# Two-stage kernel on one core: halved first loads, squares by ScalarE, and a newly searched order of all steps

## The chip, the cores and the metric

The kernel runs on one core of one Trainium2 chip. A core has a matrix engine (TensorE, PE in the profile, with its weight loads as PEld), a vector engine (VectorE, DVE), an engine for activations (ScalarE, ACT), a general one (GpSimd, POOL) and one that here only issues DMAs (SyncE, SP). Each engine works through its own list of instructions in order; semaphores make one engine wait for another. The metric is the device time of one execution in microseconds (us); lower is better.

## The reference

Attention over chosen blocks, followed by a Fourier mix and a two-layer network with one activation. The inputs are q, k and v (4 batches, 8 heads, 768 positions, 64 wide, float32), and two weight matrices (512 x 2048 and 2048 x 512).

```python
k_rep = k.reshape(B, H, 12, 64, D).mean(axis=3)          # one mean key for each block of 64
gate = einsum('bhsd,bhnd->bhsn', q, k_rep), future blocks at -1e9
mask = (block is own or among the top 3 of gate) and causal
attn = softmax(where(mask, q k^T / 8, -1e9));  x = attn v  # heads side by side: 4 x 768 x 512
u  = x + real(fft2(x))                                    # over positions and over the 512 columns
un = (u - mean(u)) / sqrt(var(u) + 1e-6)                  # over the 512 columns
out = u + relu(un @ w_ch1) @ w_ch2
```

## The kernel before

Two heads of one batch make a pair; there are 16 pairs, four to a batch. For each pair the kernel turns q and k (for pairs 0 to 6 by PE transposes, for the later ones by DVE transposes), sums k over blocks, finds for each query the third largest gate score, and turns the comparison into a mask that is added to the scores by matmuls. The scores are held transposed (keys on partitions) in six tiles for a pair, and ScalarE takes their exponential; GpSimd cuts the causal diagonal; a second matmul with v and a column of ones gives the result and the sum.

When the four pairs of a batch are done, the Fourier part follows: folds (additions and subtractions on DVE), a cosine and sine transform over positions (`y`), copies by ACT or DVE (`ty`, `tr`), a transform over columns (`m`), then u = x + that, its mean and variance, a scaled copy of u, and its transpose `unT`. W1 and W2 follow. For batches 0 and 1 W2 is a plain product; for batches 2 and 3 it is done in seven block products in place of eight (sums and differences of blocks on DVE: steps `T` and `S`, products `p`, additions `po`).

No loop sets the order. A long string, `ORDER`, holds one word for each step of each pair, batch and tile, and a loop at the end calls the steps in that order; each engine's own order follows from it. `name:numbers` is a step with its pair or batch and tile, `@n` says which of a few buffers it takes, and `~` picks the other of the two engines that a step knows (for `qc`, `qs`, `vc`, `qm`, `qn`: ACT in place of DVE or GpSimd). The words that matter here:

- `Lq`, `Lk`, `Lv`: loads by SP. `tq`, `tk`: PE transposes of q and k (`a_tp`, L320); `tj`: of the last third of k of pair 0 (`b_tp`, L327).
- `ks`, `kj`: sums of k over blocks on DVE (L390, L331). `qc`: copy of q in float32 (L239 on ACT, L241 on DVE); `qs`, `kc`, `kd`: q and k as float16.
- `g`, `gj`: gate matmuls (L433, L344). `gt`, `tg`, `gx`, `xg`, `gl`, `lg`, `gm`, `mg`: turning, top three, comparison and turning back on DVE. `g`, `gt`, `gx`, `go`, `gl`, `gm` serve the first five of pair 0's nine gated blocks of 64 queries (for other pairs all of them), `gj`, `tg`, `xg`, `og`, `lg`, `mg` its other four.
- `s`, `e`, `d`: scores (L527, L532, with the mask's matmuls at L539), exponential (L549), diagonal (L555). `vc`: v as float16. `v`, `x`: attention times v (L567) and its division (L250).
- `fs`, `fd`, `f`, `fe`: folds. `y`, `ty`, `tr`, `m`, `u` (L691): the transform and u with its sum of a row. `bn`, `nv`, `nr`: statistics of a row, first guess of the inverse root and its refinement. `xu`, `xv`: scaled copy. `xt`, `un`: transpose, on PE for batch 0, by transposing DMAs on SP (L742) for the others.
- `w`, `r`: W1 and its relu (L801, L803; L811, L813). `c`, `o`: W2 of batches 0 and 1 (L820, L826). `od`: store (L832).

`consts_first` stands ahead of the string. It issues the loads of pair 0 (L903: q in two DMAs, one on SP and one on ACT's queue, then k likewise), makes constants on GpSimd and DVE, and lets PE run eight matmuls on a tile of zeros (L914). q of pair 0 is turned as a whole, k in two parts of four and two blocks of 128 rows.

The variance of all batches comes from `n_stats` (two instructions on DVE for each of six tiles of a batch, L747 and L748), and `n_guess` reads it.

Of the kernel before, what the change touches and what calls it, by code (L numbers as in the profile page):

```python
# [11 lines left out]
FP = mybir.dt.float32  # L12
F16 = mybir.dt.float16
# [93 lines left out]
Lq:1@1 Lk:1@1 tq:0@1 Lk:2@2 tk:0@2 ~qc:0@0 tj:0@3 ks:0 Lq:2@2 kj:0 kc:0 g:0@0 gj:0@1 kd:0 gt:0  # L107
tq:1@2 ~qs:0 tg:0 Lq:3@0 gu:0 xg:0 tk:1@0 og:0 gx:0 ~qc:1@1 go:0 lg:0 gl:0 mg:0@0 s:0,5@3 gm:0
s:0,2@1 ks:1 Lk:3@0 qs:1 e:0,5@0 s:0,4@2 e:0,2 ~kc:1 g:1@3 e:0,4 s:0,1@1 gt:1 s:0,0@0 ~gu:1 e:0,1
tk:2@3 gx:1 d:0,4 tq:2@2 go:1 gl:1 e:0,0 Lv:0@0 ks:2 s:0,3@1 Lq:4@1 ~qc:2@0 gm:1@1 tq:3@0 ~kc:2  # L110
e:0,3 qs:2 g:2@2 Lk:4@1 s:1,2@3 gt:2 ~qc:3@1 s:1,0@1 ~gu:2 tk:3@2 gx:2 e:1,2@1 qs:3 go:2 s:1,1@0
ks:3 e:1,0 d:0,2 s:1,4@3 Lv:1@1 d:0,5 ~kc:3 d:0,3 e:1,1 Lq:5@2 vc:0 tq:4@1 e:1,4 g:3@2 d:0,0 qc:4@0
d:0,1 Lk:5@2 s:1,3@0 gl:2 s:1,5@3 ~qs:4 tk:4@1 gt:3 gm:2@2 e:1,3 ~gu:3 v:0@2 d:1,4 ks:4 e:1,5 gx:3
kc:4 s:2,3@0 vc:1 go:3 x:0 s:2,0@3 e:2,3@0 Lv:3@0 s:2,4@1 d:1,5 d:1,3 e:2,0 g:4@2 gl:3 d:2,3 fs:0,1
Lv:2@1 tq:5@0 fs:0,0 e:2,4 gm:3@3 d:2,0 Lk:7@0 gt:4 d:1,0 tk:5@3 d:1,2 ~qc:5@1 d:1,1 s:2,5@2 ~kc:5
s:2,1@1 d:2,4 e:2,5 s:2,2@0 ~gu:4 e:2,1 vc:3 ks:5 v:1@2 e:2,2 qs:5 gx:4 s:3,5@1 go:4 s:3,0@3 gl:4
e:3,5@1 d:2,2 x:1 s:3,2@0 e:3,0 Lq:6@0 d:3,5 g:5@1 vc:2 e:3,2 s:3,3@2 gt:5 Lk:6@1 d:2,1 gm:4@0
s:3,1@3 d:3,0 gu:5 s:3,4@1 e:3,3 gx:5 d:2,5 v:2@0 d:3,2 kb:7 LT:0 e:3,1 W:0 Lq:7@1 fs:1,0 ~go:5
e:3,4 s:4,4@2 x:2 d:3,1 s:4,2@3 d:3,3 e:4,4@0 s:4,0@1 d:3,4 gl:5 v:3@0 fs:2,0 gm:5@1 e:4,2 fs:2,1
fs:1,1 e:4,0 s:5,2@2 x:3 s:4,5@3 e:5,2@1 s:4,1@1 fd:2,1 s:4,3@0 fs:3,0 e:4,5 s:5,3@2 fs:3,1 e:4,1  # L120
fd:2,0 s:5,5@3 fd:3,1 e:5,5 tq:6@1 fd:3,0 e:4,3 ~fe:0,3 s:5,0@3 f:0,2 e:5,3 tk:6@0 ~fe:0,0 ~fe:0,2
f:0,0 ~qc:6@0 s:5,4@2 LF:0 f:0,1 fe:0,1 ks:6 e:5,4 y:0,0@1 qs:6 Lv:4@0 f:0,3 e:5,0 Lc:0 pg:0 ks:7
d:4,0 g:6@2 d:4,1 ty:0,0 d:4,2 y:0,1@3 gt:6 Lv:5@1 d:4,5 ~tr:0,0 d:5,2 gu:6 gx:6 Lk:8@2 d:4,3
s:5,1@2 W:1 go:6 gl:6 ~tr:0,1 qc:7@1 m:0,2@1 vc:4 ty:0,1 gm:6@2 d:4,4 kc:6 m:0,0@3 d:5,0 u:0,2@0
d:5,4 e:5,1 Lk:9@1 d:5,3 v:4@0 qs:7 u:0,0@1 xu:0,2 s:6,4@1 xv:0,2 x:4 vc:5 m:0,1@2 kh:7 e:6,4@0
d:5,5 s:6,1@3 u:0,1@2 d:5,1 s:6,3@0 e:6,1 xt:0,2@1 ~xu:0,0 g:7@2 xv:0,0 ~xu:0,1 v:5@3 e:6,3 gt:7
un:0,2 ~gu:7 W:2 ~xv:0,1 xt:0,0@2 s:6,5@1 un:0,0 xt:0,1@0 e:6,5 s:6,0@1 un:0,1 Lq:9@2 s:6,2@2 e:6,0
x:5 w:0,8@0 d:6,0 bn:0,0 w:0,1@1 r:0,8 gx:7 kc:7 go:7 w:0,5@3 gl:7 gm:7@3 K:7 kb:8 w:0,6@0 r:0,5
ks:8 r:0,1 bn:0,3 w:0,3@3 r:0,6 d:6,3 bn:0,5 e:6,2 w:0,12@1 r:0,3 Lq:8@0 s:7,5@0 s:7,0@2 ~r:0,12
e:7,5@1 s:7,4@3 kh:8 e:7,0 s:7,3@0 fs:4,1 w:0,0@1 qc:9@0 e:7,4 Li:0 Lv:6@0 kb:9 e:7,3 w:0,10@2 qs:9  # L130
# [24 lines left out]
v:10@3 fs:11,1 r:1,8 Lv:12@1 d:12,1 fs:11,0 s:13,5@0 s:13,3@1 x:10 e:13,5@0 w:1,11@2 e:13,3 d:13,5
fs:10,1 fd:11,1 s:13,1@0 r:1,11 fd:11,0 s:13,2@3 fs:10,0 w:1,7@1 e:13,1 fd:10,1 go:14 fd:10,0
e:13,2 gl:14 s:13,4@2 f:2,2 w:1,3@0 ~fe:2,0 e:13,4 gm:14@2 d:13,2 ~fe:2,3 f:2,3 d:13,1 kh:15
w:1,14@3 f:2,1 r:1,7 K:14 qc:15@1 s:12,4@2 r:1,14 ~fe:2,2 f:2,0 w:1,0@1 e:12,4 nv:1 s:13,0@3 fe:2,1
~r:1,3 y:2,0@2 e:13,0 ~r:1,0 d:13,0 s:12,2@0 d:13,3 pg:2 g:15@3 e:12,2 d:13,4 y:2,1@1 gt:15 vc:13
tr:2,0 d:12,0 s:12,3@3 Lv:14@0 gu:15 nr:1 gx:15 ty:2,0 c:1,0,0@0 go:15 gl:15 e:12,3 ~ty:2,1 v:13@2  # L160
~tr:2,1 ~qs:15 m:2,0@3 d:12,3 x:13 d:12,2 qs:14 m:2,2@1 gm:15@3 kc:15 u:2,0@0 c:1,1,0 d:12,4 d:12,5
bn:2,0 vc:12 s:14,1@2 u:2,2@2 s:14,0@3 K:15 c:1,0,1 e:14,0@0 bn:2,4 e:14,1 bn:2,1 s:14,2@1 d:14,0
bn:2,5 s:14,4@3 e:14,2 c:1,1,1 e:14,4 ~vc:14 v:12@2 o:1,1 o:1,0 od:1,1 s:15,0@1 nv:2,2 od:1,0
s:15,5@3 c:1,4,0@0 e:15,5@1 e:15,0 xu:2,2 x:12 d:15,0 s:15,3@3 d:14,2 s:14,3@1 nv:2,0 un:2,2 e:15,3
c:1,4,1 fs:13,1 e:14,3 xu:2,0 d:15,3 fs:13,0 d:14,4 s:14,5@2 d:14,1 m:2,1@3 o:1,4 e:14,5 d:15,5
s:15,1@1 od:1,4 u:2,1@1 d:14,3 s:15,2@2 e:15,1 c:1,5,0 bn:2,2 e:15,2 d:15,1 d:14,5 bn:2,3 s:15,4@3
# [30 lines left out]
def kernel(  # L197
# [34 lines left out]
    def pick(a, b):  # L232
        return b if other[0] else a
# [778 lines left out]
```

## Time and profile before

| | us |
|---|---|
| median of 3 runs (lowest, highest) | 277.81 (277.69, 278.2) |
| the profiled execution | 277.79 |
| its span in the trace | 276.1 |
| PE busy | 267.9 |
| DVE busy | 221.5 |
| ACT busy | 178.3 |
| POOL busy | 107.4 |

The span runs from the first instruction of the program to the last one; the time of the execution is 1.7 us more. Busy time is the time in which at least one instruction of an engine runs. Rows of a group name the line, engine and operation, what is written and read, the shape and the count; then busy time in us and the mean length of one in ns, then how long the engine stood still just before these and what ended that.

### The profile page before, as it was taken

What the parts mean: (1) busy time and instruction counts of PE and PEld (TensorE: products, weight loads), DVE (VectorE), ACT (ScalarE), POOL (GpSimd) and SP (SyncE); (2) the same over time, 40 slices, a digit from 0 to 9 for tenths busy, and PEclk for the clock granted to TensorE, in tenths of its full rate; (3) what the DMA queues carried; (4) which work ended last, traced back from release to release, by engine and by line L of the source; (5) the groups of instructions that cost most, each with busy time, mean ns of one, the idle gap of its engine ahead of it and who ended that gap; (6) DMA issues with size and microseconds to landing.
All of it is one profiled execution on the core that took longest, in us unless ns stands there. A gap on an engine that the chain in (4) does not pass through costs nothing.

```text
span 276.1 us, 7004 instructions
## 1 busy us (share of the span) xinstructions
PE 267.9 (97%) x2660; PEld 181.2 (66%) x2660; DVE 221.5 (80%) x683; ACT 178.3 (65%) x243; POOL 107.4 (39%) x304
## 2 busy tenths in 40 slices
PE   8899989999999999999999999999999999999995
PEld 4566766765576565666665755655766888666884
DVE  1888999998789889899789797879999894307883
ACT  3799999969999759978799687802546310274100
POOL 5155927634783476405976691520100011000000
PEclk9999999999999999999999999999999999999999
DMA  8999999998799999479471202351100412300025
GB/s 190 271 229 235 186 233 207 180 153 151 134 174 189 168 188 194 115 124 234 119 149 29 57 2 78 77 105 51 38 2 0 59 19 68 127 0 2 0 112 194
DMA packets 121138, 33.47 MB, mean 121 GB/s; under 512 B 113616, under 2 KB 118160, under 8 KB 121104
## 3 DMA queue, kind: packets, MB, share of 16 engines
q1 hardware_dynamic: 115872, 28.43, 48.1%
q0 software_dynamic: 3664, 4.19, 9.8%
q10 hardware_dynamic: 1568, 0.39, 0.6%
q8 instruction: 21, 0.34, 0.5%
q14 instruction: 13, 0.11, 0.1%
HBM read 28.55 MB, written 6.29 MB: 126 GB/s over the span
## 4 chain that ended last, share of the span: by engine, by line
PE 81%; DVE 6%; ACT 5%; POOL 2%; issue 2%; SPq 2%; DMA 1%; DVEq 0%; ACTq 0%; POOLq 0%
PE h L801 19%; PE cw L879 13%; PE c L820 12%; PE h L803 9%; PE sc L532 7%; PE av L567 5%; PE tp L320 2%; ACT pt L549 2%; PE yp L639 2%; PE sc L527 2%; PE mx L672 2%; SPq L742 2%; PE mx L673 2%; PE sc L539 1%; PE warmps L914 1%
## 5 line engine op out<-in xcount | busy, mean ns | idle before, releaser
L549 ACT ACTIVATE pt<-sc 128x1024 f16<-128x1024 f32 (+1 forms) x96 | 83.4, 925 | 12.1 <-PE sc L532 8.1
L801 PE MATMUL h<-unT,w 128*128 128x512 f16 x256 | 84.6, 379 | 0.3 <-DMA unT<-x 0.3
L803 PE MATMUL h<-unT,w 128*128 128x256 f16 x256 | 69.7, 272 | 0.0
L813 ACT ACTIVATE hT<-h 128x768 f16<-128x768 f32 x50 | 39.4, 811 | 41.1 <-PE h L803 40.7
L555 POOL TENSOR_SCALAR_AFFINE_SELECT pt<-pt 128x256 f16<-128x256 f16 x96 | 37.4, 413 | 21.0 <-ACT pt L549 19.9
L820 PE MATMUL c<-w_sb,hT 128*128 128x512 f16 x192 | 44.5, 379 | 0.0
L801 PEld LDWEIGHTS <-w 128*128 128x128 f16 x256 | 25.0, 98 | 29.7 <-issue 1.4
L820 PEld LDWEIGHTS <-hT 128*128 128x128 f16 x192 | 18.3, 98 | 20.3 <-issue 0.5
L253 POOL TENSOR_SCALAR_AFFINE_SELECT qk<-mt 32x160 f16<-32x160 f16 x72 | 23.9, 353 | 18.2 <-DVE mt L504 16.7
L803 PEld LDWEIGHTS <-w 128*128 128x128 f16 x256 | 25.0, 98 | 3.6
L532 PE MATMUL sc<-qk 96*128 96x512 f16 (+3 forms) x144 | 26.1, 305 | 0.0
L567 PEld LDWEIGHTS <-pt 128*128 128x128 f16 x672 | 22.3, 97 | 3.2 <-ACT pt L549 0.7
L567 PE MATMUL av<-v,pt 128*128 128x65 f16 x672 | 23.2, 193 | 0.3 <-ACT pt L549 0.3
L253 POOL TENSOR_SCALAR_AFFINE_SELECT qk<-q 64x768 f16<-64x768 f32 (+1 forms) x15 | 12.3, 822 | 22.8 <-ACT q L239 15.3
L886 DVE SCALAR_TENSOR_TENSOR u<-cw,rt,u 128x256 f32<-128x256 f32 x35 | 16.6, 480 | 4.7 <-PE cw L879 4.1
L879 PEld LDWEIGHTS <-s 128*128 128x128 f16 x192 | 18.8, 98 | 2.2
L532 PEld LDWEIGHTS <-qk 96*128 96x128 f16 x144 | 13.1, 98 | 7.8
L811 DVE TENSOR_SCALAR hT<-h 128x768 f16<-128x768 f32 x14 | 13.3, 956 | 4.0 <-PE h L803 3.9
L879 PE MATMUL cw<-w2t,s 128*128 128x256 f16 x144 | 16.4, 273 | 0.0
L250 DVE TENSOR_TENSOR s<-hT,hT 128x384 f16<-128x384 f16 x16 | 5.4, 354 | 13.4 <-ACT hT L813 13.3
L250 DVE TENSOR_TENSOR x<-av,rcp 128x768 f16<-128x768 f32 x16 | 15.3, 958 | 0.6
L879 PEld LDWEIGHTS <-hT 128*128 128x128 f16 x144 | 14.1, 98 | 2.0
(155 smaller groups left out, 457.2 us busy)
## 6 DMA issues: line engine op xcount, KB each, us to landing
nat<-in_v_dram SPq DMA_DIRECT2D x16, 384.0 KB, 4.6
out_dram<-u SPq DMA_DIRECT2D x20, 256.0 KB, 2.4
nat<-in_k_dram SPq DMA_DIRECT2D x36, 96.0 KB, 3.4
nat<-in_q_dram SPq DMA_DIRECT2D x36, 96.0 KB, 2.9
nat<-in_q_dram SPq DMA_DIRECT2D x13, 192.0 KB, 3.7
nat<-in_k_dram SPq DMA_DIRECT2D x13, 192.0 KB, 3.9
w_sb<-in_moe_w_ch_dram POOLq DMA_DIRECT2D x2, 1024.0 KB, 11.2
w<-in_moe_w_ch_dram POOLq DMA_DIRECT2D x2, 768.0 KB, 7.1
```

The source lines that it names most:

```text
L250: (eng or nc.vector).tensor_tensor(out=out, in0=in0, in1=in1, op=op)
L253: nc.gpsimd.affine_select(out=out, in_=in_, pattern=[[0, i] for i in n], base=0, channel_multiplier=0, compare_op=ALU.is_ge, fill=0.0)
L532: nc.tensor.matmul(ps[:, e, co:co + q1 - q0], qk[0:96, e, 1, 128 * jt:128 * jt + 128], qk[0:96, e, 0, q0:q1], start=True, stop=True)
L549: nc.scalar.activation(out=d["pt"][:, o:o + 2 * n].rearrange("p (e c) -> p e c", e=2), in_=d["sc", i][:, :, 0:n], func=AF.Exp, scale=0.125)
L555: nc.gpsimd.affine_select(out=dg, in_=dg, pattern=[[0, 2], [1, 128]], base=0, channel_multiplier=-1, compare_op=ALU.is_ge, fill=0.0)
L567: nc.tensor.matmul(av[:, e, 66 * st:66 * st + 65], pt[:, co:co + 128], vv[:, e, jt, 0:65], start=(cnt == 0), stop=(cnt == 20))
L801: nc.tensor.matmul(hp[:, 0:512], w1s, unT[:, dt, 0:512], start=(dt == 0), stop=(dt == NDT - 1))
L803: nc.tensor.matmul(hp[:, 512:768], w1s, unT[:, dt, 512:768], start=(dt == 0), stop=(dt == NDT - 1))
L813: nc.scalar.activation(out=hT, in_=hp, func=AF.Relu)
L820: nc.tensor.matmul(c_ps[b, g[0]][:, st - g[0], :], h_t[b, it][:, 128 * st:128 * (st + 1)], w2_sb[:, it, :], start=(it == 0), stop=(it == N ...
L879: nc.tensor.matmul(o, x, y, start=(i == 0 and W7_FIRST[n]), stop=(i == 7), skip_group_check=True)
L886: nc.vector.scalar_tensor_tensor(out=o, in0=c_ps[b, "w", st][:, W7_BANK[n], 0:256], scalar=rt_t[b][:, kt:kt + 1], in1=o, op0=ALU.mult, op1 ...
```

## The change

The change has four parts.

1. **First pair.** q of pair 0 is loaded and turned in two parts as k is: eight DMAs in place of four, first four blocks of 128 rows of k and of q (each on SP and ACT's queue), then the other two blocks of k and q, all on SP. New steps `tn`, `qn` and `qm` turn and copy the second part of q; `tq`, `qc` and `qs` of pair 0 handle 512 columns. k now comes ahead of q.
2. **Warm-up.** The tile of zeros is 128 columns wide and read four times by each matmul; there are seven matmuls in place of eight, and the copy that reads their result moves to the end of DVE's constants.
3. **Variance of batches 2 and 3.** `bn` is replaced by two steps: `mn` scales the sum of a row that `u` left to minus the mean (DVE, two columns at a time), and `sq` lets ACT square u minus mean and sum the row; the squares themselves are written over x, which is not read any more. `n_guess` divides the sum by 512. Batches 0 and 1 keep `bn`.
4. **Order.** All steps stand in a new order, with other buffers and other choices of engine here and there: q of pair 4 is copied by ACT in place of DVE, two casts of v move from GpSimd to ACT, one copy of `tr` from DVE to ACT, two relus from ACT to DVE.

```diff
     def a_tp(P, who):
-        two = P == 0 and who == 1
+        two = P == 0
...
+    def b_tq(P):
+        pairs[P]["tpn"] = ps = pst([128, 256], f"tpn_{P}")
+        src = nat[P, 0].rearrange("p st e d -> p st (e d)")
+        for st in range(4, NST):
+            nc.tensor.transpose(ps[:, 128 * st - 512:128 * st - 384], src[:, st, :], id32)
+
+    def b_q32(P):
+        conv(pick(nc.vector, nc.scalar), q_tile(P)[:, 512:S], pairs[P]["tpn"], None)
+
+    def b_q(P):
+        conv(pick(nc.gpsimd, nc.scalar), qk_s[P % NSLOT][:, 0, XW(P), 512:S], q_tile(P)[:, 512:S], [S - 512])
...
+    def n_mean(b, kp):
+        sm = st_t[b][2][:, 2 * kp:2 * kp + 2]
+        nc.vector.tensor_scalar(out=sm, in0=sm, scalar1=-1.0 / DM, scalar2=None, op0=ALU.mult)
+
+    def n_square(b, kt):
+        nc.scalar.activation(out=x_t[b][:, kt, :], in_=u_t[b, kt // 2][:, kt % 2, :], func=AF.Square,
+                             bias=st_t[b][2][:, kt:kt + 1], accum_out=st_t[b][0][:, kt, 1:2])
...
-            nc.vector.tensor_scalar(out=vr, in0=mv[:, :, 1], scalar1=1e-6, scalar2=None, op0=ALU.add)
+            nc.vector.tensor_scalar(out=vr, in0=ss, scalar1=1.0 / DM, scalar2=1e-6, op0=ALU.mult, op1=ALU.add)
...
-            nc.vector.scalar_tensor_tensor(out=nm, in0=mv[:, :, 0], scalar=-1.0, in1=g,
-                                           op0=ALU.mult, op1=ALU.mult)
+            tt(nm, nm, g, ALU.mult)
...
-            for e, eng in ((0, nc.sync), (1, nc.scalar)):
-                eng.dma_start(t[:, :, e, :], src[0, e].rearrange("(st p) d -> p st d", p=128))
+        for h in (slice(0, 4), slice(4, NST)):
+            for who in (1, 0):
+                src = (q, k)[who]
+                for e, eng in ((0, nc.sync), (1, nc.sync if h.start else nc.scalar)):
+                    eng.dma_start(nat[0, who][:, h, e, :],
+                                  src[0, e].rearrange("(st p) d -> p st d", p=128)[:, h, :])
...
-        for _ in range(8):
-            nc.tensor.matmul(wps, wsrc[:, 0:128], wsrc, start=True, stop=True)
+        for _ in range(7):
+            nc.tensor.matmul(wps.rearrange("p (r c) -> p r c", c=128), wsrc, wsrc.rearrange(
+                "p (r c) -> p r c", r=1).to_broadcast([128, 4, 128]), start=True, stop=True)
```

The head of the order, before and after:

```diff
-Lq:1@1 Lk:1@1 tq:0@1 Lk:2@2 tk:0@2 ~qc:0@0 tj:0@3 ks:0 Lq:2@2 kj:0 kc:0 g:0@0 gj:0@1 kd:0 gt:0
-tq:1@2 ~qs:0 tg:0 Lq:3@0 gu:0 xg:0 tk:1@0 og:0 gx:0 ~qc:1@1 go:0 lg:0 gl:0 mg:0@0 s:0,5@3 gm:0
+tk:0@1 Lq:1@1 tq:0@2 ks:0 Lk:1@1 tj:0@3 ~qc:0@0 kj:0 Lk:2@2 ~qs:0 g:0@0 tn:0@2 gt:0 ~qn:0 gu:0 gx:0
+Lq:2@2 kc:0 gj:0@0 go:0 gl:0 ~qm:0 tg:0 kd:0 gm:0@0 s:0,0@2 xg:0 Lq:3@0 og:0 tk:1@1 e:0,0@0 lg:0
```

The stretch in which batch 2 passes from attention to W1, before and after:

```diff
-s:15,1@1 od:1,4 u:2,1@1 d:14,3 s:15,2@2 e:15,1 c:1,5,0 bn:2,2 e:15,2 d:15,1 d:14,5 bn:2,3 s:15,4@3
-d:15,2 v:14@1 nv:2,1 e:15,4 ~xu:2,1 c:1,5,1 d:15,4 un:2,1 nr:2 v:15@2 o:1,5 T:2 od:1,5 c:1,2,0@3
-un:2,0 x:14 c:1,2,1 x:15 fs:12,1 fs:12,0 c:1,3,0 fs:14,1 fs:14,0 fs:15,1 fs:15,0 fd:14,1 fd:15,1
+m:2,1@1 e:15,3 un:2,2 c:1,5,0 e:15,1 u:2,1@1 s:15,2@0 mn:2,1 fs:13,0 s:14,5@2 c:1,5,1 e:14,5 e:15,2
+d:14,5 d:15,2 s:15,4@1 o:1,5 v:14@2 e:15,4 d:15,3 od:1,5 od:1,4 sq:2,3 c:1,2,0@0 d:15,4 un:2,0
+d:15,1 sq:2,2 d:15,5 nv:2,1 v:15@3 nr:2 ~xu:2,1 x:14 un:2,1 c:1,2,1 fs:14,1 x:15 c:1,3,0 fs:15,1
```

## The prediction

> **What bounds the kernel now.** I read the page's first part, then busy time by stage, the chain that ended last, the waits, and the start row by row.
>
> ```profile
> span 276.1 us, 7004 instructions
> PE 267.9 (97%) x2660; PEld 181.2 (66%) x2660; DVE 221.5 (80%) x683; ACT 178.3 (65%) x243; POOL 107.4 (39%) x304
> ```
>
> ```profile
> core 0: us, PE busy (x) PEld busy (x) DVE busy (x) ACT busy (x) POOL busy (x), PEclk, DMA share, GB/s
> 11.01:35.58 24.57, 23.62 (x412) 16.85 (x410) 22.09 (x84) 23.78 (x30) 16.44 (x41) 1.00 1.02 229
> 35.58:58.00 22.42, 21.15 (x368) 16.10 (x363) 21.31 (x64) 20.85 (x31) 11.03 (x24) 1.00 1.06 184
> ...
> 150.00:178.79 28.79, 28.79 (x291) 18.46 (x290) 23.75 (x77) 22.50 (x28) 17.48 (x49) 1.00 0.19 52
> ```
>
> ```profile
> 58.00:272.85 214.85, 214.24 (x1832) 142.78 (x1830) 172.83 (x508) 128.99 (x178) 75.74 (x216) 1.00 0.48 96
> 272.85:276.09 3.24, 0.00 (x0) 0.00 (x0) 0.48 (x1) 0.00 (x0) 0.00 (x0) 1.00 0.53 185
> ```
>
> The cuts are events: 11.01 is the first exponential, 35.58 the end of the last one of the first batch (e:3,4), 58.00 the first W1 matmul. Ahead of 58.00 PE is fed by others: ACT has 23.78 of 24.57 us filled between 11.01 and 35.58, and DVE 21.31 of 22.42 after that. From 58.00 on PE is filled to 214.24 of 214.85, and 3.24 us of last addition and store follow. So the time is a sum: first W1 matmul, plus the PE work behind it, plus PE's idle time there (0.61), plus the tail. The change leaves the matmuls behind the first W1 matmul as they are (in the built order the same PE work stands ahead of it, but for one warm-up matmul less). It can only move the first W1 matmul, and the 0.61.
>
> The profiled execution took 277.79 us, 1.7 over its span; the median of the runs is 277.81. I sum against 277.79.
>
> **The start.** Each row is start, length, engine, line, operation.
>
> ```profile
> 0.82 0.47 ACTq L903 DMA_DIRECT2D nat<-in_q_dram  x1
> 1.31 3.59 PE L914 MATMUL warmps<-zeros 128*128 128x512 f16 x8 [1.31 <-DVE zeros L911]
> 1.32 0.69 ACTq L903 DMA_DIRECT2D nat<-in_k_dram  x1
> 1.94 1.14 SPq L304 DMA_DIRECT2D nat<-in_q_dram  x2
> 4.69 2.34 PE L320 MATMUL tp<-id,nat 128*128 128x128 f32 x10
> 6.22 0.80 ACT L239 COPY q<-tp 128x768 f32<-128x768 f32 x1 [2.68 <-PE tp L320]
> 7.14 0.69 DVE L390 TENSOR_REDUCE kra<-tp 128x8 f32<-128x512 f32 x1 [1.18 <-PE tp L320]
> 7.87 0.59 ACT L239 CAST qk<-tp 128x512 f16<-128x512 f32 x1 [0.85 <-DVE kra L390]
> 7.98 0.48 PE L433 MATMUL g<-q,kra 64*32 64x160 f32 x8 [0.53 <-DVE kra L390]
> 8.35 0.38 ACT L239 CAST qk<-tpj 128x256 f16<-128x256 f32 x1
> 8.51 0.35 DVE L448 STREAM_TRANSPOSE gt<-g 128x160 f32<-128x160 f32 x1 [0.27 <-PE g L433]
> 8.74 1.53 PE L320 MATMUL tp<-id,nat 128*128 128x128 f32 x12
> 9.65 0.80 ACT L239 COPY q<-tp 128x768 f32<-128x768 f32 x1 [0.20 <-PE tp L320]
> 10.62 0.30 DVE L502 STREAM_TRANSPOSE mt<-lt 128x160 f16<-128x160 f16 x1
> 11.01 4.19 ACT L549 ACTIVATE pt<-sc 128x256 f16<-128x256 f32 x5 [0.55 <-PE sc L539]
> ```
>
> ```profile
> nat<-in_q_dram ACTq DMA_DIRECT2D x1, 192.0 KB, 3.6
> nat<-in_k_dram ACTq DMA_DIRECT2D x1, 192.0 KB, 4.4
> ```
>
> The whole q of pair 0 (384 KB) is in at 0.82 + 3.6 = 4.4, k 384 KB later at 1.32 + 4.4 = 5.7. In the new order 256 KB of k come first (about 4.0), then 256 KB of q (4.8), then the two rests (5.2 and 5.7), by the same 384 KB in 1.3 us. Four of the six issues on SP are new and stand ahead of pair 1's loads. At 0.57 each (1.14 for 2) they put pair 1's first issue from 1.94 to about 4.2. Its bytes have the same place in the stream, and its transposes, at 8.74 before, come after the first scores now; I count nothing. If that cover goes, the price is the 2.3 us that the issue slips, less what the queue hides.
>
> One warm-up matmul less (3.59 / 8 = 0.45) and a smaller zero fill let PE be free at about 4.1. The four transposes of k run from 4.25, of q from 5.1 (0.23 each, as in the ten of 2.34), the rest of k from 6.0. DVE's first sum starts at 5.4 in place of 7.14. ACT's copy of q's first 512 columns starts at 6.25, no earlier than 6.22 before, and takes 0.59 in place of 0.80. Gating matmuls of the first five blocks: 6.9 (7.98 before). Now the new link: mask part one (gm) stands on DVE behind tg, which waits for gj, which waits for ACT's ~qn, which waits for the transposes tn of q's rest, and these stand on PE behind g. With tn done at about 7.8, ~qn 0.38 (the 256 columns at 8.35), gj and tg like g and its turn (0.48 and 0.35) and gm 0.30, the mask is there at about 9.3. With an estimate of 0.6 for the mask's matmuls and the hand-overs the first exponential starts at 9.9 (9.6 to 10.6), 1.1 sooner.
>
> **What ACT pays for it.** Behind its first exponential ACT has, up to e:3,4, the same 24 exponentials in both orders, but two copies of 768 columns more: q of pair 1 (before, it ran at 9.65, ahead of the first exponential), and q of pair 4, which moves from DVE.
>
> ```profile
> L241 DVE COPY q<-tp 128x768 f32<-128x768 f32 x1 | 1.0, 959 | 0.0
> L250 DVE TENSOR_TENSOR sd<-x 128x384 f16<-128x384 f16 x32 | 11.2, 383 | 0.0
> L747 DVE BATCH_NORM_STATS2 bst<-u 128x6 f32<-128x512 f32 x22 | 14.8, 674 | 0.0
> L748 DVE BATCH_NORM_AGGREGATE mv<-bst 128x2 f32<-128x6 f32 x24 | 4.4, 182 | 0.8
> L727 ACT ACTIVATE x<-u,nm 128x512 f16<-128x512 f32 x7 | 4.9, 720 | 0.2
> L549 ACT ACTIVATE pt<-sc 128x1024 f16<-128x1024 f32 x80 | 78.5, 1032 | 8.2 <-PE sc L532 5.8 <-POOL v L253 0.8 <-PE sc L539 0.6
> ```
>
> Two copies at 0.8 are +1.6. ACT's own waits in that stretch were 24.57 - 23.78 = 0.79; I let 0.4 of them go (bounds 0 and 0.79). So e:3,4 moves by -1.1 + 1.6 - 0.4 = **+0.1** (from -0.6, with the first exponential at 9.6 and no waits, to +1.2). The second half of ACT's gain is already spent: that is why I don't carry the 1.1 to the end.
>
> From e:3,4 to the first W1 matmul DVE carries the folds, sums and copies. In the new order one fold (0.38) more lies on this side; DVE waited 22.42 - 21.31 = 1.1 in this stretch, and I let 0.4 of that go: **0.0** (-0.7 to +0.4). DVE's saving ahead of it (0.96 for the copy, and a first sum 1.7 us sooner) doesn't count, since DVE then waits for the same exponentials.
>
> **The variances.** For batches 2 and 3, twelve statistics and twelve aggregates leave DVE (12 x (0.67 + 0.18) = 10.3 us) and twelve Square activations with a sum go to ACT. No row shows one. Nearest is L727, the same tile by ACT at 0.72; with a sum to read out I take 0.8, bounds 0.72 and 1.03 (an exponential of twice the width). ACT gets 9.6 us. DVE also gets six scalings for six multiplications kept; nothing on the path. Four squares of batch 2 stand ahead of the last exponential, 3.2 us against ACT's idle 28.79 - 22.50 = 6.3 there: hidden. If they were not, e:15,4 would be late, and v:15 and W1 of batch 2 behind it. Two more stand behind the last exponential, where PE has four blocks of W2 and one of attention queued. DVE's relief sets nothing free where PE is already full.
>
> Square's table is a price that only a page states. The Trainium skill (ScalarE: Activation LUTs, "Table sets: the hidden batching unit") doesn't list square beside exp, and has each switch of sets cost 2.66 us; by it, as an estimate, squares alternating with exponentials would add over 20 us. The built order of the change holds one table load, as before, so the sum takes none.
>
> **PE's idle time behind 58.00.** Two waits make most of it, and the chain of work gives the prices around the second:
>
> ```profile
> 141.26 0.91 PE L567 MATMUL av<-v,pt 128*128 128x65 f16 x24 [0.30 <-ACT pt L549]
> 187.47 0.38 PE L801 MATMUL h<-unT,w 128*128 128x512 f16 x1 [0.27 <-DMA unT<-x]
> ```
>
> ```profile
> 167.56 1.28 PE av L567 x42
> ...
> 171.99 1.73 PE c L820 x8
> ...
> 184.84 2.50 DMA unT<-x
> ```
>
> Ahead of the first, two casts of v move from POOL to ACT; ahead of the second, the transposing DMAs of batch 2's first third no longer stand last behind a store on SP. I take -0.3 for the two (bounds -0.6, all of it, and +1.0, a new wait like those before 58.00). Tail: the last three additions and stores are the same; 0.
>
> **Sum:** 277.79 + 0.1 + 0.0 - 0.3 = **277.6 us**: no change that can be measured.
>
> **Rivals.**
> Faster: the new order takes all waits that rows show. ACT's 0.79 vanishes (another -0.4), DVE's 1.1 too (-0.7 at most, I take half, -0.35), and PE's 0.61 (another -0.3): 276.6. For it: DVE has 1.7 us and a copy in hand, so masks come early and ACT need not wait for scores. Against it: ACT has 1.6 more to do.
> Slower: the squares delay the last exponentials. It decides once ACT is more than about 1.5 us behind at s:15,4 (PE then holds 4 x 1.73 + 2 x 1.28 = 9.5 us of work; the way by e:15,4, two squares, variance and x, a first transposing DMA's issue, an estimate of 1.3, and the next one's landing is some 8.0: 1.0 + 1.6 + 1.6 + 1.3 + 2.5). With most of the squares' 3.2 not hidden ACT is 2.5 late and PE stands 1.0: 278.6. For it: ACT's idle time there is in front of scores that PE delivers late. Against it: 6.3 exceeds 3.2.
> The start doesn't do what it says: q's second half lands late behind six issues on SP, or PE still runs at its first pace (0.23 a transpose in the ten at 4.69, 0.13 in the twelve at 8.74, while the clock column says 1.00). First exponential at 10.6: 278.3. The Trainium skill (TensorE: Matmul & The Clock Gate, "Part 1: The HAM clock gate") has the half rate last through a window of some 3.4 us that isn't tied to the kernel's start; the two paces agree with a half rate.
>
> **How the numbers follow.** No change that counts 0.40, faster rival 0.28, slower rival 0.22, start fails 0.10. About 0.2% (0.55 us) is what a measurement of this kernel can tell from no change, so the bounds are 277.25 and 278.35. Faster takes 0.9 of its rival and a fifth of my forecast (0.33); slower 0.75 of its rival, half of the last and a tenth of my forecast (0.27); the rest is 0.40. Range 276.5 to 278.7: the faster rival to the slower one; my forecast alone spans 277.1 to 278.1.
>
> **What would show it.** First exponential near 9.9; e:3,4 ending near 35.7; first W1 matmul near 58.1; PE idle behind it under 0.6; twelve squares near 0.8. I am wrong if the first W1 matmul is before 57.4, or if PE waits for av or unT over 1 us near 180.

## The result, and the profile after

The change makes the kernel slower: 281.17 us median (279.63 to 282.71, 4 runs) against 277.75 (277.68 to 278.2, 4 runs) on the same chip, a ratio of 1.0125 with a 95% interval of 1.0094 to 1.0155. The executions also lie further apart: over 3 us, against 0.5 before (2.8 in the 30 executions of before beside e13 to e16). The profiled one is the fastest of the four (279.63, span 277.9), so its rows show only part of the loss. The other spans are 278.6, 280.2 and 281.0.

The first part of the page of after, and its busy time by the same stages (columns: window; length, then the busy time and count of PE, PEld, DVE, ACT and POOL; granted clock; DMA share; GB/s). The cuts are the first exponential, the end of e:3,4, the first W1 matmul, the end of the last matmul, and the end:

```profile
span 277.9 us, 7017 instructions
PE 268.2 (97%) x2659; PEld 181.0 (65%) x2659; DVE 212.1 (76%) x667; ACT 187.3 (67%) x269; POOL 105.5 (38%) x302
```

```profile
9.13:35.39 26.26, 25.56 (x424) 18.42 (x425) 21.95 (x86) 25.17 (x32) 15.52 (x37) 1.00 1.02 229
35.39:58.87 23.48, 21.48 (x367) 16.16 (x364) 21.71 (x66) 21.37 (x30) 10.68 (x28) 1.00 1.09 193
58.87:274.10 215.23, 214.36 (x1832) 142.95 (x1830) 163.72 (x490) 136.63 (x201) 75.60 (x216) 1.00 0.47 96
274.10:277.88 3.78, 0.00 (x1) 0.00 (x0) 0.48 (x1) 0.00 (x0) 0.00 (x0) 1.00 0.42 147
```

| mark, us | before | after | forecast |
|---|---|---|---|
| first exponential | 11.01 | 9.13 | 9.9 |
| e:3,4 ends | 35.58 | 35.39 | 35.7 |
| first W1 matmul | 58.00 | 58.87 | 58.1 |
| PE idle behind it | 0.61 | 0.87 | 0.3 |
| tail | 3.24 | 3.78 | 3.24 |

The start gained more than forecast, and nearly all of it was gone at e:3,4, as forecast. Then 0.87 is lost up to the first W1 matmul, 0.4 behind it and 0.5 in the tail: 1.8 in all. Each column of marks is one execution. Before's first exponential is a late one: six other profiles with the same first pair (e2, e3, e8, e11, e13 and e16, below) have it at 10.44 to 10.59, so the start gained some 1.4 rather than 1.9.

The waits of PE in after (engine, line, what is waited for: us in total, times, longest) name two for POOL's diagonals, in one row, and one for a load of k, none of which before has:

```profile
PE av L585 <- POOL pt L573: 1.5, 2, 0.8
PE tp L321 <- DMA nat<-in_k_dram: 0.4, 1, 0.4
```

The first of POOL's two is v:3, where PE waits 0.71 up to 37.19. The timeline of POOL in after shows why (start, length, engine, line, operation, idle ahead of it and what ended it):

```profile
32.71 1.32 POOL L573 TENSOR_SCALAR_AFFINE_SELECT pt<-pt 128x256 f16<-128x256 f16 x3
35.35 0.95 POOL L970 DMA_DIRECT2D w<-in_moe_w_ch_dram  x1 [1.33 <-issue]
36.34 0.41 POOL L573 TENSOR_SCALAR_AFFINE_SELECT pt<-pt 128x256 f16<-128x256 f16 x1
```

POOL is ready at 34.03 (32.71 + 1.32) and next on its queue is `W:0`, the issue of the load of the first W1 block, for which the kernel sets no semaphore to wait for. It begins 1.33 us later all the same, and pair 3's last diagonals stand behind it. Before, this issue came at 33.71, with no idle ahead of it.

The second is v:11 at 142, with a wait of 0.75. Two diagonals took 1.76 us together, the second of them 1.41 where others take 0.41, beside four folds in a row on DVE:

```profile
141.05 1.76 POOL L573 TENSOR_SCALAR_AFFINE_SELECT pt<-pt 128x256 f16<-128x256 f16 x2
```

```profile
141.41 1.14 DVE L251 TENSOR_TENSOR sd<-x 128x384 f16<-128x384 f16 x4
```

### The profile page after: what moved, and what is told of

Its sections match the earlier page's. It is cut to its first block, busy times and chain, and to the rows that moved or that the text cites. A ratio compares the mean times of both kernels' runs of the same rounds, so it can differ in the third digit from the quotient of the medians.

```text
span 277.9 us, 7017 instructions
## 1 busy us (share of the span) xinstructions
PE 268.2 (97%) x2659; PEld 181.0 (65%) x2659; DVE 212.1 (76%) x667; ACT 187.3 (67%) x269; POOL 105.5 (38%) x302
## 4 chain that ended last, share of the span: by engine, by line
PE 79%; ACT 11%; DVE 2%; SPq 2%; POOL 2%; DMA 1%; issue 1%; POOLq 0%; ACTq 0%
PE h L826 18%; PE c L845 15%; PE cw L904 13%; PE h L828 9%; ACT pt L567 7%; PE sc L550 6%; PE av L585 5%; PE yp L657 2%; PE tp L321 2%; PE mx L690 2%; PE mx L691 2%; PE sc L545 1%; DMA nat<-in_k_dram 1%; PE sc L557 1%; SPq L930 1%; PE g L459 1%
## 5 line engine op out<-in xcount | busy, mean ns | idle before, releaser
L838 ACT ACTIVATE hT<-h 128x768 f16<-128x768 f32 x48 | 37.5, 808 | 37.0 <-PE h L828 26.9
L573 POOL TENSOR_SCALAR_AFFINE_SELECT pt<-pt 128x256 f16<-128x256 f16 x96 | 38.5, 422 | 50.6 <-ACT pt L567 49.7
L826 PEld LDWEIGHTS <-w 128*128 128x128 f16 x256 | 25.0, 98 | 28.4 <-issue 0.7
L845 PEld LDWEIGHTS <-hT 128*128 128x128 f16 x192 | 18.2, 98 | 20.2 <-issue 0.5
L254 POOL TENSOR_SCALAR_AFFINE_SELECT qk<-mt 32x160 f16<-32x160 f16 x72 | 23.2, 342 | 10.4 <-DVE mt L522 7.3
L836 DVE TENSOR_SCALAR hT<-h 128x768 f16<-128x768 f32 x16 | 15.1, 948 | 4.1 <-PE h L828 3.8
L709 DVE SCALAR_TENSOR_TENSOR u<-mx,x 128x512 f32<-128x512 f32 x22 | 14.1, 684 | 3.1 <-PE mx L691 3.1
L851 DVE SCALAR_TENSOR_TENSOR u<-c,rs,u 128x512 f32<-128x512 f32 x12 | 8.8, 744 | 9.3 <-PE c L845 9.3
L251 POOL TENSOR_TENSOR vr<-vr,rs 128x6 f32<-128x6 f32 x4 | 1.1, 267 | 38.1 <-DVE rs L788 37.9
```

What stands on the lines that cost most here:

```text
L251: (eng or nc.vector).tensor_tensor(out=out, in0=in0, in1=in1, op=op)
L254: nc.gpsimd.affine_select(out=out, in_=in_, pattern=[[0, i] for i in n], base=0, channel_multiplier=0, compare_op=ALU.is_ge, fill=0.0)
L573: nc.gpsimd.affine_select(out=dg, in_=dg, pattern=[[0, 2], [1, 128]], base=0, channel_multiplier=-1, compare_op=ALU.is_ge, fill=0.0)
L826: nc.tensor.matmul(hp[:, 0:512], w1s, unT[:, dt, 0:512], start=(dt == 0), stop=(dt == NDT - 1))
L838: nc.scalar.activation(out=hT, in_=hp, func=AF.Relu)
L845: nc.tensor.matmul(c_ps[b, g[0]][:, st - g[0], :], h_t[b, it][:, 128 * st:128 * (st + 1)], w2_sb[:, it, :], start=(it == 0), stop=(it == N ...
```

## The experiments

All of them compute the whole of the reference. Times are medians of 4 to 12 executions, and the ratio is to before, run between them on the same chip (before's medians were 277.57 to 277.80). "Number" is the place of `W:0` in POOL's built stream, and three columns are read from that kernel's profile: "stand" is POOL's idle time ahead of `W:0`, "first W1" the start of the first W1 matmul, "packet" the start of a packet of instructions that is explained below. e5's profile, of an execution of 394.62 us, can't be compared.

| run | what it is | ratio (95%) | number | stand, us | first W1, us | packet, us |
|---|---|---|---|---|---|---|
| before | | 1 | 58 | 0 | 58.00 | 29.2 |
| after | | 1.0125 (1.0094 to 1.0155) | 57 | 1.33 | 58.87 | 33.0 |
| e1 | after up to un:0,1, then before | 1.0131 (1.0096 to 1.0167) | 57 | 2.39 | 61.34 | 34.2 |
| e2 | before up to un:0,1, then after | 1.0110 (1.0089 to 1.0131) | 58 | 0 | 58.91 | 28.7 |
| e3 | before with squares | 1.0055 (1.0043 to 1.0067) | 58 | 0 | 57.61 | 28.9 |
| e4 | before with after's start | 1.0068 (1.0049 to 1.0086) | 58 | 0 | 59.04 | 30.8 |
| e5 | after, W:0 behind d:3,4 | 1.0056 (1.0032 to 1.0081) | 59 | - | - | - |
| e6 | after, Lc:0 later | 1.0083 (1.0052 to 1.0114) | 57 | 2.07 | 60.09 | 33.5 |
| e7 | after without squares | 1.0226 (1.0183 to 1.0270) | 57 | 2.31 | 59.51 | 34.2 |
| e8 | after with before's start | 1.0033 (1.0014 to 1.0053) | 59 | 0 | 58.04 | 28.4 |
| e9 | after, two memsets at the start | 1.0049 (1.0031 to 1.0068) | 59 | 0 | 57.71 | 28.7 |
| e10 | after, W:0 ahead of d:3,3 | 1.0124 (1.0106 to 1.0143) | 57 | 1.74 | 60.44 | 34.8 |
| e11 | before, five selects on POOL behind W:0 | 1.0070 (1.0049 to 1.0091) | 59 | 0 | 59.25 | 28.4 |
| e12 | e4, buffers renamed | 1.0027 (1.0013 to 1.0042) | 58 | 0 | 58.45 | 29.6 |
| e13 | before, one POOL memset fewer | 1.0014 (0.9985 to 1.0043) | 57 | 0 | 58.99 | 29.7 |
| e14 | e9, four folds later | 1.0076 (1.0047 to 1.0106) | 59 | 0 | 57.98 | 28.6 |
| e15 | before, after's warm-up | 1.0013 (0.9993 to 1.0032) | 58 | 0 | 58.87 | 29.6 |
| e16 | before, squares for batch 3 alone | 1.0019 (0.9992 to 1.0046) | 58 | 0 | 59.01 | 29.8 |
| e17 | after, one memset at the start | 1.0081 (1.0060 to 1.0102) | 58 | 0 | 59.15 | 28.3 |
| e18 | after, two memsets ahead of W:0 | 1.0103 (1.0081 to 1.0125) | 59 | 0.36 | 58.97 | 33.9 |

No version is faster than before.

The marks vary from one execution to the next: before, e3 and e16 have the same words up to the first W1 matmul, and it comes at 57.6 to 59.0. Compare with that the kernels with after's order around `W:0`. With a stand of 1.33 or more (after, e6, e7, e10) the first W1 matmul comes at 58.9 to 60.4, 59.7 on average, and without it or with 0.36 of it, behind the same start (e9, e14, e17, e18), at 57.7 to 59.2, 58.5 on average. The difference of 1.3 is rough, with four profiles on each side.

### Two halves of the change: e1 and e2

```text
 ORDER (e1) = after's words up to un:0,1, then before's words not yet issued (bn)
 ORDER (e2) = before's words up to un:0,1, then after's words not yet issued (mn, sq)
```

> After's code and order up to the copy un:0,1 just ahead of the first W1 matmul, before's order with bn variances from there on. Theory A (the loss is where the two profiles part: 0.85 us at the first W1 matmul, 0.44 behind it, 0.50 in the tail): first W1 matmul near 58.9, 278.6 us. Theory B (the loss is the squares and the new order behind the first W1 matmul): 277.8 or less. Theory C (the new order of the first 58 us is what makes the executions spread from 279.6 to 282.7): 280 to 281 with a spread of over 2 us.

> The complement: before's start and order up to un:0,1, after's order with squares from there on. Theory A: first W1 matmul near 58.0, 278.7 us. Theory B: 280 to 281. Theory C: 278 to 279 with a spread under 1 us.

e1 took 280.81 us (279.95 to 283.15), e2 280.46 (279.96 to 281.9). Theory A falls: each half costs almost as much as the whole. e1 came out where theory C put it, e2 where theory B did. But the halves don't add up, since each has a seam: just ahead of the first W1 matmul PE waits 1.1 for an exponential, in e1 and in e2 alike. What e1 gave is the view of an execution that is not the fastest. Its waits of PE up to 62, its POOL and DVE around `W:0`, and its stages of 2 us:

```profile
PE av L583 <- POOL pt L571: 1.8, 1, 1.8
PE sc L543 <- ACT pt L565: 1.1, 1, 1.1
```

```profile
36.12 0.95 POOL L969 DMA_DIRECT2D w<-in_moe_w_ch_dram  x1 [2.39 <-issue]
```

```profile
34.58 0.96 DVE L249 TENSOR_TENSOR x<-av,rcp 128x768 f16<-128x768 f32 x1
37.60 0.43 DVE L249 TENSOR_TENSOR lt<-gt,mx 128x108 f16<-128x108 f32 x1 [2.07 <-POOL gt L508]
```

```profile
36.00:38.00 2.00, 0.22 (x8) 0.10 (x5) 0.40 (x2) 1.83 (x3) 1.85 (x5) 1.00 0.86 146
38.00:40.00 2.00, 2.00 (x42) 1.55 (x44) 1.97 (x7) 0.00 (x0) 0.30 (x1) 0.78 0.96 131
40.00:42.00 2.00, 1.95 (x30) 1.69 (x25) 2.00 (x6) 1.86 (x4) 0.00 (x0) 0.50 1.26 219
42.00:44.00 2.00, 2.00 (x35) 1.41 (x34) 2.00 (x10) 1.89 (x3) 0.00 (x0) 0.87 1.16 324
44.00:46.00 2.00, 1.88 (x19) 1.44 (x20) 2.00 (x5) 2.00 (x3) 0.00 (x0) 1.00 1.26 277
```

With a stand of 2.39, PE idles 1.78 us ahead of v:3, and then runs at a lower granted clock from 38 to 44: (0.22 + 0.50 + 0.13) x 2 = 1.7 us of full clock, which is 3.4 us at half. So a stand costs twice, by this one profile, and the second time only in some executions: after's span of 281.0 had a mean clock of 0.985. Among executions under 290 us, means under 0.990 are seen in after, e1 and e7 alone, all with a stand. A mean just under 1 need not be such a loss: in e17's profile (mean 0.996) every stretch of 2 us from 10 us to 276 has 1.00, and only the time behind the last matmul (274.4) less. Nor is the clock the whole spread: after's span of 280.2 had a mean clock of 1.00. The Trainium skill (TensorE: Matmul & The Clock Gate, "Part 1: The HAM clock gate") has the clock fall after an idle window of some 3.4 us that runs freely, and rise again after a busy one as long. The 3.4 us at half rate agree; the fall after only 1.78 us of idle time does not, and here the measurement decides.

### The squares: e3, e16 and e7

```diff
-u:2,0 ... bn:2,0 bn:2,4 bn:2,1 ...          (e3, batch 3 likewise; e16: batch 3 alone)
+u:2,0 ... mn:2,0 sq:2,0 mn:2,2 sq:2,4 sq:2,1 ...
-mn:2,0 ... sq:2,0 sq:2,5 sq:2,1 ...         (e7: the opposite, in after)
+bn:2,0 bn:2,5 bn:2,1 ...
```

> Before with the variances of batches 2 and 3 by ScalarE squares, each square where the statistics stood, all else as before. Theory A: 277.8 (the squares take ScalarE time that it has idle). Theory B: over 278.6, with exponentials of batch 3 late. Rival that the DVE relief helps: under 277.3.

> Before with squares for batch 3 alone, batch 2 by bn as before. e3 with both cost 1.3 us; in its profile the last exponential and the first W1 matmul of batch 2 came 1.0 us late. If batch 2's squares ahead of the last exponentials are the whole price: 277.7. If batch 3's cost as well: 278.3 or more.

> After with bn_stats and bn_aggr of batches 2 and 3 in place of each square, same places. From e3 the squares cost 1.0 us in before's order (last exponentials late, first W1 matmul of batch 2 at +1.0). If after's order has hidden them: the same 281 as after. If they cost in after's order too: about 1 us less, 280. If DVE needs the relief there: slower, 282 or more.

e3 took 279.01 us (278.95 to 279.26), 1.3 more than before; e16, with batch 3 alone, 278.04 us, which can't be told from before. So by the medians batch 2's squares carry most of the price. ScalarE in e3 ahead of the last exponentials, and what PE then waits for:

```profile
176.03 0.72 ACT L749 ACTIVATE x<-u,sm 128x512 f16<-128x512 f32 x1
176.66 0.19 ACT L749 ACTIVATION_READ_ACCUMULATOR x<-u,sm 128x1 f32 x1
176.75 1.00 ACT L548 ACTIVATE pt<-sc 128x1024 f16<-128x1024 f32 x1
177.66 0.71 ACT L749 ACTIVATE x<-u,sm 128x512 f16<-128x512 f32 x1
178.27 0.19 ACT L749 ACTIVATION_READ_ACCUMULATOR x<-u,sm 128x1 f32 x1
178.36 1.01 ACT L548 ACTIVATE pt<-sc 128x1024 f16<-128x1024 f32 x1
```

```profile
PE h L807 <- DMA unT<-x: 1.1, 1, 1.1
```

A square with its sum takes 0.72 + 0.19. Two of them stand between the last exponentials, e:15,4 comes 1.0 late (counted from the first W1 matmul of the kernel), and the first W1 matmul of batch 2 waits 1.1 for its transposed input (0.3 before). In after's order it is the other way round: without squares (e7) the kernel takes 283.83, some 2.7 us more than after. Between the first W1 matmuls of batches 2 and 3, here e7 and then after:

```profile
191.68:234.74 43.06, 40.71 (x311) 29.90 (x311) 38.25 (x105) 15.22 (x21) 2.62 (x12) 1.00 0.13 34
```

```profile
190.50:230.43 39.93, 39.93 (x311) 29.93 (x310) 34.23 (x96) 19.21 (x33) 2.72 (x12) 1.00 0.18 37
```

PE is idle for 2.35 there in e7, in four waits for DVE's additions of W2, and not at all in after: its order packs other DVE work into the time that the squares free. It has hidden them and needs them.

### The start alone: e4, e12, e8 and e15

```text
 ORDER (e4)  = after's words up to e:0,3, then before's; after's loads and warm-up, bn
 ORDER (e12) = the same; before's buffers @0 @1 @2 @3 of PSUM renamed to @2 @0 @3 @1
 ORDER (e8)  = before's words up to e:0,3, then after's; before's loads and warm-up
-        for _ in range(8):                      (e15: this alone, in before)
+        for _ in range(7):                      (and the zeros 128x128, cleared first)
```

> Before with the halved loads and transposes of the first pair and after's order up to the exponential e:0,3; before's order and bn variances behind it. If the start's gain (first exponential 9.13 in place of 11.01) is kept by before's order, first W1 matmul near 57.2 and 277.0 us. If it is lost again because the keys of the next pair land later (9.4 in place of 8.5) and ScalarE pays two copies more: first W1 matmul 57.9 to 58.2, 277.8 us. If the loss of the change comes with the start itself: 278.6 or more.

> The kernel of e4 with the PSUM buffers of the grafted rest renamed to fit (in e4 g:2 shared its buffer with the transposes of q of pair 3, and PE stood 1.24 us for ScalarE's copy of them, ScalarE 1.30 us behind it). Without that stand e4's 279.44 becomes 278.2. If the start's gain (first exponential 9.03 in place of 11.01) then reaches the end: 277 or less; if it is spent on ScalarE's two copies more, as I predicted: 277.6 to 278.2.

> After's order and squares from e:0,3 on behind before's whole first pair (loads, transposes, copies not halved). Theory D (POOL's stand comes with after's order around W:0, not with the start): stand and spread stay, 280.5 to 282. Rival (the early start is what makes W:0 collide with saturated queues): no stand, 278.5 to 279.3.

> Before with after's warm-up alone (zeros of 128x128, cleared first, seven matmuls in place of eight). PE is free 0.8 us sooner, q of pair 0 lands at 4.4. If the start is set by PE's slow first pace until it speeds up: no change, 277.6. If by the warm-up in front of the first transposes: first exponential near 10.3 and 277.2 us. If the shorter warm-up leaves PE slow for longer: 278 or more.

e4 took 279.44 us, e12 278.33: first exponentials at 9.03 and 9.06, first W1 matmuls at 59.04 and 58.45 (58.00 before). The start alone brings the first exponential some 1.4 us sooner and gains nothing: e12 is 0.7 us slower than before, e4 1.9. PE's instructions stand in the same order in both; what the renaming changes is their waits. This one of e4, for the copy of q of pair 3, is not in e12:

```profile
PE g L449 <- ACT q L238: 1.2, 1, 1.2
```

So the conflict of buffers was there and the renaming removes it; its price of 1.1 is less sure, since the two intervals just part. e8, after's order behind before's start, took 278.96 us: of the 3.5 us (1.25% of 277.75) 0.9 is left, with a spread of 1.2. e15 (278.27 us) can't be told from before; its first exponential, at 10.37, is no more than 0.2 ahead of those with before's warm-up (10.44 to 10.59), so the start's gain is not the warm-up's.

### The stand ahead of W:0: e5, e6, e10, e9, e17, e18 and e13

```diff
-d:3,2 kb:7 e:3,1 d:3,3 Lc:0 W:0 e:3,4 ... d:3,1 ... d:3,4 gl:5
+d:3,2 kb:7 e:3,1 d:3,3 Lc:0 e:3,4 ... d:3,1 ... d:3,4 W:0 gl:5   (e5)
+d:3,2 W:0 kb:7 e:3,1 d:3,3 Lc:0 e:3,4 ...                         (e10)
+d:3,2 kb:7 e:3,1 d:3,3 W:0 e:3,4 ...      (e6: Lc:0 ahead of pg:0)
         nc.gpsimd.memset(kra, 0.0)
+        nc.gpsimd.memset(gone, 0.0)       (e9: twice; e17: once; e18: twice, ahead of W:0)
-        nc.gpsimd.memset(kra, 0.0)        (e13, in before)
+        nc.vector.memset(kra, 0.0)
```

> After with one token moved: the software DMA for the first W1 block (W:0) is issued on POOL behind d:3,4 in place of ahead of d:3,1. In the profile of after POOL stands 1.33 us with no wait shown before that issue, in e1 2.39 us, and v:3 on PE waits for the diagonals behind it (0.9 and 1.78 us); in e1 the granted clock then falls to 0.78, 0.50 and 0.87 from 38 to 44 us. Theory D (that stand, and the clock that falls behind it in some executions, is the spread and most of the loss): v:3 does not wait for POOL, no stretch under clock 1.00, spread under 1 us, 278.6 to 279.3 us. Rival (the stand goes with the stage and not with the issue, or the issue now holds batch 1's diagonals): 280.5 or more and the same spread.

> After with one token moved: the two index loads Lc:0 leave SP's queue just ahead of W:0 and go where before had them (ahead of pg:0). If POOL's issue of W:0 stands because SP's issues of Lc stand just ahead of it: no stand, 278.6 to 279.3 us. If Lc has nothing to do with it: POOL's issue gap stays at 1.3 to 2.4 us and the time at 280 to 282.

> After with W:0 one diagonal earlier on POOL, behind d:3,2 as in before. If place 57 of the stream is what stands: it is still 57, so d:3,3 and d:3,1 come 1 us late or more and the time stays at 280 to 282. If W:0 stands because of the queues at 34 us: it is ready 0.6 us earlier, the same or a longer stand, 280 to 282. If neither (the stand belongs to issuing right behind two diagonals in a row): no stand, 278.5 to 279.3.

> After with two tiny POOL memsets (4 elements) more among the constants at the start, where POOL has nothing to do; all else the same. They move every later POOL instruction two places down its stream. POOL's issue of W:0 stood 1.3 to 2.4 us, with no wait shown, in the four profiles where it is number 57 of the built POOL stream, and 0 in those where it is 58 or 59. If the place in the stream makes the stand: no stand ahead of W:0, 278.5 to 279.3 us. If W:0 stands because of what the DMA queues hold at that time: the stand of 1.3 us or more stays, 280 to 282 us.

> Before with one POOL memset of the constants (kra) given to DVE, nothing else: W:0 goes from place 58 of POOL's stream to 57, where it stood in after. If the place alone makes the stand: 1.3 to 2.4 us of idle POOL with no wait shown ahead of W:0, pair 3's diagonals late, 279 to 281 us. If place and after's order are both needed: no stand, 277.6 us as before.

> After with one tiny POOL memset among the constants in place of e9's two: W:0 at place 58 of POOL's stream. If only place 57 stands: no stand ahead of W:0, 278.5 to 279.3 us. If e9's gain needs both: stand of 1.3 us or more, 280 to 282.

> After with e9's two tiny memsets directly ahead of W:0, so that the start is as in after and W:0 is at place 59. If the place in the stream decides: no stand, 278.5 to 279.3 us. If e9's start decides: stand of 1.3 us or more, in front of the memsets or of W:0, 280 to 282 us.

The stand stays without SP's loads `Lc:0` ahead of it (e6: 280.27 us, stand 2.07) and with `W:0` one diagonal earlier (e10: 281.05 us, stand 1.74). With `W:0` behind d:3,4 (e5) the kernel is 1.6 us slower than before, about 1.9 faster than after; its other eleven executions still lie 2.5 apart, where I had expected under 1. Two memsets of four elements, far ahead and in idle time, take it away: in e9 POOL goes on at once,

```profile
33.97 0.95 POOL L972 DMA_DIRECT2D w<-in_moe_w_ch_dram  x1
```

v:3 no longer waits, and the kernel takes 278.99 us (278.54 to 279.74). In after's order the five profiles with `W:0` at number 57 have stands of 1.33 to 2.39, and of five at 58 or 59 four have none and e18 has 0.36. But the place alone is not the cause: before's order has no stand at 57 either (e13, 278.23 us, not to be told from before), nor in any of its nine profiles.

The traces hold one more sign. Their DMA view lists queues that carry instructions. For after, from 32 to 38 us, it has this row (packets, MB, share of 16 engines):

```profile
q14 instruction: 1, 0.01, 1.4%
```

The packet starts at 33.0 and takes 1.3 us; e9 has no such row there. Each profile but e5's has one such packet between 28 and 35 us, and the last column of the table gives its start. In the six profiles with any stand it comes at 33.0 to 34.8, and `W:0` begins 1.7 to 3.1 behind it; in the 13 others it comes at 28.3 to 30.8, and `W:0` begins 3.8 or more behind it. That fits a POOL that stands because its next instructions have not yet arrived, and a shift in the stream that has them asked for sooner. It is not shown: the profile does not say which engine the packet was for, and no run changed it alone.

The time does not follow the stand as closely as e9 suggested. e17 and e18 are slower than I expected of a kernel without it (278.5 to 279.3). With after's start and order, the kernels with the stand average a ratio of 1.0111 (after, e6, e10), those without it or with 0.36 of it 1.0073 (e5, e9, e14, e17, e18): 1.1 us apart, where after and e9 are 2.1 apart. In e18 and in e17 PE waits for other things ahead of the first W1 matmul. Waits of PE up to 60 us, e18 and then e17:

```profile
PE tp L320 <- DMA nat<-in_q_dram: 1.0, 1, 1.0
PE tp L320 <- DMA nat<-in_k_dram: 0.4, 1, 0.4
```

```profile
PE av L585 <- POOL v L254: 0.8, 1, 0.8
```

```profile
49.95 0.90 POOL L254 TENSOR_SCALAR_AFFINE_SELECT v<-nat 128x768 f16<-128x768 f32 x1 [1.48 <-DMA nat<-in_v_dram]
```

In e18 (280.54 us) PE waits 1.0 for a load of q; in e17 (279.90 us) POOL waits 1.48 for a load of v, and PE 0.8 for its cast. The stages up to 58 us have a DMA share of 1.02 and 1.09 in after (1.02 and 1.06 before), so the loads fill the queues there. That an earlier start meets them there fits these waits; no run tests it.

### The price of a stand, and the folds: e11 and e14

```diff
-e:3,1 W:0 Lq:7@1 fs:1,0 ...                    (e11, in before)
+e:3,1 W:0 Z:5 Lq:7@1 fs:1,0 ...                (Z:5: five selects on a scratch tile, 2.27 us)
-r:1,8 fs:11,0 s:13,5@2 v:10@1 ... fs:9,0 fs:11,1 ... fs:9,1 ... x:10   (e14, in e9)
+r:1,8 s:13,5@2 v:10@1 ... x:10 fs:11,0 fs:9,0 fs:11,1 fs:9,1
```

> Before with 2.0 us of POOL work on a scratch tile (5 selects of 0.41) behind W:0, so that pair 3's last diagonals come late as in e1. Its output is the reference's. If such a stand is what costs after its time: v:3 waits over 1 us, the clock falls below 1.00 between 38 and 44 us in some executions, first W1 matmul 1 to 3 us late, 279 to 281 with a spread over 1.5 us. If the stand is only worth its own length, hidden in part: under 278.7 with a spread under 0.7.

> The kernel of e9 (278.99) with four folds on DVE (fs:11,0, fs:9,0, fs:11,1, fs:9,1) moved behind x:10. In after and in e9 a POOL diagonal took 1.40 us in place of 0.41 while these four ran on DVE one after another, and PE waited 0.8 for it. If the folds hold POOL back: the diagonal takes 0.41, PE's wait of 0.8 goes, 278.2 us. If something else slows that diagonal: 279.0 as e9, PE still waits.

e11 took 279.70 us (278.95 to 280.17), 1.9 more than before. Its waits of PE up to 62 us and its stage of v:3:

```profile
PE av L567 <- POOL pt L555: 1.7, 1, 1.7
```

```profile
36.00:38.00 2.00, 0.33 (x11) 0.28 (x10) 1.50 (x5) 1.78 (x2) 1.66 (x5) 1.00 1.34 232
```

The five selects took 2.27 us (34.13 to 36.40). So POOL's time ahead of pair 3's last diagonals arrives at the end nearly whole, 1.9 of 2.27, in before too. The spread rose to 1.2 and not over 1.5; one of six executions had a mean clock of 0.992.

e14 shows the folds' part right and its gain wrong. In its profile the two diagonals take 0.77 in place of 1.76, and PE's wait for POOL is gone; another of 1.2 for an exponential, at 149, takes its place:

```profile
140.17 0.77 POOL L572 TENSOR_SCALAR_AFFINE_SELECT pt<-pt 128x256 f16<-128x256 f16 x2
```

```profile
PE sc L549 <- ACT pt L566: 1.2, 1, 1.2
```

At 279.77 us e14 is no faster than e9; their intervals overlap. That POOL is held while such folds run agrees with the Trainium skill (SBUF — State Buffer, "SBUF: two separate sides"), by which a VectorE operation with two inputs in that memory and a GpSimd operation that reads it lock each other out, whichever starts first. Its rule that a VectorE operation in a mode that takes both ports holds up a DMA issued by GpSimd would be a cause for the stand, but does not cover e1: there DVE ends its work at 35.54 (34.58 + 0.96) and does nothing up to 36.12, when `W:0` begins.

## Why the prediction was wrong, point by point

- **Start.** Forecast 9.9 (9.6 to 10.6), measured 9.13, outside the bounds, by the mechanism given: tn is done at 7.20 (7.8 forecast), the mask at 8.72 (9.3). The price of the loads' slip that "I count nothing" for exists: PE waits 0.4 for k of pair 1, and ScalarE 0.79 behind its first exponential:

```profile
10.95 1.02 ACT L567 ACTIVATE pt<-sc 128x1024 f16<-128x1024 f32 x1 [0.79 <-PE sc L557]
```

- **What ACT pays.** Forecast +0.1 at e:3,4, measured -0.19. The mechanism is right: from the first exponential to e:3,4 ScalarE is busy 25.17 in place of 23.78 and idle 1.09 in place of 0.79, which spends 1.7 of the 1.9 gained. The waits of which I let 0.4 go did not go but grew by 0.3. That the sum comes so near is in part luck: a start 0.8 better than forecast against waits 0.7 worse.
- **From e:3,4 to the first W1 matmul.** This is the step that failed: "0.0 (-0.7 to +0.4)" was +1.06 in after's fastest execution. I gave this stage to DVE alone. v:3 hangs on POOL's diagonals, and I priced nothing on POOL's queue there: not the issue of `W:0` that stands among them in both orders (0.95 before, with no idle ahead of it), and not what a wait of PE there does to the clock. e11 sizes the first (1.9 us for 2.27 us of POOL time), e1 the second (up to 1.7). Over the profiles the first W1 matmul comes 1.3 later with the stand than without it, and without it (58.5 on average) where before's words have it too (57.6 to 59.0). In after PE's longest wait of the stage is for POOL (0.7); the longest for DVE is 0.3.
- **Squares.** 0.8 each was 0.91, within the bounds. "Hidden" is right in after's order (no wait of PE for unT) and wrong in before's (e3): there the slower rival's mechanism and its price of 1.0 came true. That a missing relief of DVE could cost 2.7 in the new order was not seen; I had said it sets nothing free. After's trace has one table load, at 1.96, so the over 20 us for switches of sets did not come.
- **PE's idle time behind 58.00.** The wait for unT went as forecast; the one for av near 141 (0.30 for ScalarE) became one of 0.8 for POOL at v:11. Idle is 0.87 in place of 0.3: within the bounds (-0.6 to +1.0), with the wrong sign. The stage is steady: 215.23 or 215.24 in the profiles of after, e6, e8, e9, e10 and e17, against 214.85.
- **Tail.** Forecast 0, measured +0.5. With after's ending it averaged 3.9 in ten profiles, with before's 3.6 in nine, each spread over 0.5 to 0.8; so 0.3 to 0.4 is the change's and the rest is spread.
- **Sum and range.** The terms behind the first W1 matmul, 0.4 and 0.3 to 0.5, make 0.7 to 0.9 (e8 measured 0.9). The other 2.6 of 3.5 come with the early start in the new order. The stand carries 1.1 (mean) to 2.1 (e9) of it. The rest is not settled; the late loads of e17 and e18 are what their rows show. My range was built on one execution, of which the first W1 matmul alone moves by 1.4 from one profile to another, and had no place for a cost that comes in some executions only. Of the chances, the terms given for a slower kernel add up to 0.255, not 0.27.
- **Rivals.** The faster one is out. The slower one named a right mechanism for before's order, but not what decided. The start did not fail.

What holds `W:0` stays open. The runs exclude `Lc:0`, the neighbouring diagonal and the place in the stream by itself; a late packet of instructions goes with it in every profile that can be compared.

## What to carry to other kernels

A DMA issue on a compute engine's queue is a step with a price of its own, in place and in variance: keep it away from work that the matrix engine waits for. A wait of the matrix engine of some 2 us can cost almost the same again in clock, so judge a wait by the executions it can spoil and not only by its length. And time gained at the head of a stage is worth nothing at its end if the work of the engine that fills the stage grows by as much: here 1.7 of 1.9 went into ScalarE's copies and waits. And a profile is one execution: here the same words put the first W1 matmul at 57.6 in one and at 59.0 in another.

## What was not expected of the hardware

- An issue of a software DMA on POOL with no wait of its own began 1.33 to 2.39 us late in five profiles, and at once when two memsets of four elements had been put far ahead of it. In the profiles with a stand, and in no other, a packet of instructions on a DMA queue came 1.7 to 3.1 us ahead of the issue, not 3.8 or more.
- The granted clock fell to half for some 3.4 us after 1.78 us of idle PE (e1); after 1.7 us in e11 it stayed at 1.00 in the profiled execution.
- A POOL select took 1.41 us in place of 0.41 beside four f16 additions on DVE that ran one after another.
